# Pooling of batch 0 reordered, the sums of E folded by GpSimd, and the first linear-term operand built earlier

## The chip, the cores and the metric

The kernel runs on one core of a Trainium2 chip. The metric is the device time of one execution in microseconds. A profile of one execution gives the traces. A run's mean clock is the mean granted clock of TensorE.

Engines are named as in the profile: PE is TensorE's matmul, PEld its weight load, DVE is VectorE, ACT is ScalarE, POOL is GpSimd. Every run of the experiments is marked as in the fast state, so fast runs are compared with fast runs throughout. A line number such as L543 is a line of the kernel profiled; the same statement has another number in another kernel.

## The reference, cut to what matters

```python
def mab(q, kv):                      # attention of q on kv
    s = scale * (q @ kv.transpose(0, 2, 1))
    a = np.exp(s - s.max(-1, keepdims=True)); a /= a.sum(-1, keepdims=True) + 1e-09
    return a @ kv
h = mab(inducing, x)                 # pooling: 32 rows h for each of 4 batches
y = mab(x, h)                        # x: 4 x 12544 x 128
out = np.maximum(y @ w1, y @ w2) @ w_out      # 128 -> 1024 -> 128
```

The kernel uses max(a, b) = a + relu(b - a). The linear term, y @ w1 @ w_out, needs only a small matrix per batch (m1, and its block-diagonal form m1d); the relu term needs hwd = h @ (w2 - w1). So each batch is pooled to h, h is turned into hwd and m1, and then the large part runs: a *burst* of matmuls, relu evictions of four PSUM banks by DVE and ACT (the matmuls write into PSUM; an eviction reads a bank out and frees it: at 97.76 us of the profile before, PE has waited 0.32 us for a relu eviction of DVE), and *finals*, groups of sixteen 128x128 matmuls. Batches 1 to 3 are pooled between the bursts of the batch before. Batch 0 has nothing to hide behind.

Of the kernel before, what the change touches and what calls it, by code (L numbers as in the profile page):

```python
# [10 lines left out]
F32 = mybir.dt.float32  # L11
# [40 lines left out]
def kernel(  # L52
# [9 lines left out]
    nc = tc.nc  # L62
    B, N, C = x.shape
    M = inducing.shape[0]
# [5 lines left out]
    P1B = 16  # L70
# [4 lines left out]
    for i, (_, n) in enumerate(p1_blocks):  # L75
        step = 8 if i == NP1 - 2 else n
        units += [(i, g, min(step, n - g)) for g in range(0, n, step)]
    units = units[:-3] + units[-1:] + units[-3:-1]
    NU = len(units)
# [5 lines left out]
    smp = ctx.enter_context(tc.tile_pool(name="smp", bufs=2))  # L85
# [8 lines left out]
    model = Model()  # L94
# [14 lines left out]
    def xn_of(b, i):  # L109
        return xn_tiles[(NP1 * b + i) % NXN]  # L110
# [45 lines left out]
    with tc.manual_schedule(engines={ET.PE, ET.DVE, ET.Activation, ET.Pool, ET.SP}):  # L156
# [21 lines left out]
        st = [dict() for _ in range(B)]  # L178
# [4 lines left out]
        def u_transpose(i):  # L183
            t, g0, n = units[i]
            xn = xn_of(0, t)
            step = 4 if i == NU - 1 else 8
            for g in range(g0, g0 + n, step):
                m = min(step, g0 + n - g)
                bi, ps = bank([128, 8, 128], F16)
                end = 0.0  # L190
                for j in range(m):
                    nc.tensor.transpose(ps[:, j, :], xn[:, g + j, :], identity16)  # L192
                    end = model.pe(0.056)
                k = p1_blocks[t][0] + g
                dst = xT_tiles[0][:, k : k + m, :]
                if (g // step) % 2 == 0:
                    nc.vector.tensor_copy(out=dst, in_=ps[:, 0:m, :])  # L197
                    model.bank_free[bi] = model.ev("DVE", 64 * m, end)
                else:
                    nc.scalar.copy(out=dst, in_=ps[:, 0:m, :])  # L200
                    model.bank_free[bi] = model.ev("ACT", 128 * m, end)

        def u_scores(i):
            t, g, n = units[i]
            k = p1_blocks[t][0] + g
            bi, ps = bank([128, P1B * M])
            for j in range(n):
                nc.tensor.matmul(
                    out=ps[:, j * M : (j + 1) * M],
                    lhsT=xT_tiles[0][:, k + j, :],  # L210
                    rhs=inducingT,
                    start=True,
                    stop=True,
                )
                end = model.pe(0.025, model.bank_free[bi])
            et = etp.tile([128, P1B, M], F16, name=f"et_0_{i}", tag="et")
            nc.scalar.activation(
                out=et[:, 0:n, :], in_=ps[:, 0 : n * M], func=AF.Exp, scale=scale
            )
            model.bank_free[bi] = model.ev("ACT", n * M, end)  # L220
            pool0["et", i] = et
# [96 lines left out]


        def small_fold(b):  # L320
            es = smp.tile([128, 1, M], F32, name=f"esum_{b}", tag="esum")
            nc.vector.reduce_sum(  # L322
                out=es[:, 0, :],
                in_=st[b]["eacc"].rearrange("p k m -> p m k"),
                axis=mybir.AxisListType.X,
            )
            model.ev("DVE", P1B * M, 0.0)
            st[b]["esum"] = es[:, 0, :]

        def small_h(b):  # L330
            es = st[b]["esum"]
# [36 lines left out]
        mask = consts.tile([128, 4, 1], F16, name="mask")  # L368

        def small_m1(b):  # L370
            bi, ps = bank([128, 512])
            nc.tensor.matmul(
                out=ps[:, 0:128], lhsT=st[b]["hT4"], rhs=w1out, start=True, stop=True
            )
            end = model.pe(0.06, model.bank_free[bi])
            m1, m1d = m1_tiles[b % 2], m1d_tiles[b % 2]
            nc.scalar.copy(out=m1, in_=ps[:, 0:128])
            model.bank_free[bi] = model.ev("ACT", 128, end)
            nc.gpsimd.tensor_mul(
                m1d,  # L380
                m1[:, None, :].broadcast_to((128, 4, 128)),
                mask.broadcast_to((128, 4, 128)),
            )
            st[b]["m1"], st[b]["m1d"] = m1, m1d


# [55 lines left out]
        class Part:  # L442
# [6 lines left out]
                self.nburst = NJB // self.jpb // (2 if blk.dup else 1)  # L449
                self.name = f"{blk.name}_{t0}"  # L450

            def burst(self, u, lead=()):

                blk, w, jpb = self.blk, self.w, self.jpb
                if u == 0:
                    self.relu = relup.tile(
                        [128, NJB, blk.g, self.tn, 128], F16, name=f"relu_{self.name}", tag="relu"
                    )
                banks = []
                end = 0.0  # L460
                for q in range(4):
                    bi, ps = bank([128, 512])
                    banks.append((bi, ps, jpb * (q // 2 if blk.dup else u)))
                    free = model.bank_free[bi]
                    model.bank_free[bi] = 1e9
                    end = model.pe(0.0, max(free, blk.ready), "row")
                for jj in range(jpb):
                    for q in range(4):
                        bi, ps, j0 = banks[q]
                        jb = j0 + jj  # L470
                        r = slice(32 * q, 32 * (q + 1))
                        nc.tensor.matmul(  # L472
                            out=ps[:, jj * w : (jj + 1) * w],
                            lhsT=st[blk.b]["hwd"][r, 128 * jb : 128 * (jb + 1)],
                            rhs=blk.e2[r, 128 * self.t0 : 128 * self.t0 + w],
                            start=True,
                            stop=True,
                            tile_position=(32 * q, 0),
                        )
                end = model.pe(0.22, 0.0, "row")  # L480
                for part, q in lead:
                    part.open_final(q)
                for s in range(2):
                    for part, q in lead:
                        r = slice(32 * q, 32 * (q + 1))
                        tt = part.t0 + s
                        nc.tensor.matmul(  # L487
                            out=part.fin[q][1][:, 128 * s : 128 * (s + 1)],
                            lhsT=part.blk.e2[r, 128 * tt : 128 * (tt + 1)],
                            rhs=st[part.blk.b]["m1"][r, :],  # L490
                            start=(s == 0),
                            stop=False,
                            tile_position=(32 * q, 0),
                        )
                    if lead:
                        model.pe(0.056, 0.0, "row")
                for q in range(4):
                    bi, ps, j0 = banks[q]
                    eng = model.pick(512, end)
                    dst = self.relu[:, j0 : j0 + jpb, q % blk.g, :, :]  # L500
                    src = ps.rearrange("p (j t c) -> p j t c", j=jpb, c=128)
                    if eng == "DVE":
                        nc.vector.tensor_scalar(  # L503
                            out=dst, in0=src, scalar1=0.0, scalar2=None, op0=ALU.max
                        )
                    else:
                        nc.scalar.activation(out=dst, in_=src, func=AF.Relu)  # L507
                    self.done = model.bank_free[bi] = model.ev(eng, 512, end)
# [110 lines left out]
        def prep_w1out():  # L619
# [10 lines left out]
            nc.scalar.copy(out=w1out, in_=ps[:, 0:128])  # L630
            model.bank_free[bi] = model.ev("ACT", 128, end)

        last = NU - 3
        for i in range(last - 1):
            u_transpose(i)
            if i >= 1:
                u_scores(i - 1)
            if i >= 2:
                u_accum(i - 2)
            keep_warm(1)  # L640

        u_transpose(last - 1)
        u_scores(last - 2)
        u_transpose(last)
        u_transpose(last + 1)
        u_scores(last - 1)
        u_transpose(last + 2)
        u_accum(last - 3)
        u_scores(last)
        u_scores(last + 1)  # L650
        u_scores(last + 2)
        for i in range(last - 2, NU):
            u_accum(i)
        for i in range(NXN - NP1):
            load_x(1, i)
# [34 lines left out]
        for b in range(B - 1):  # L690
            nb, g = b + 1, first[b]
# [15 lines left out]
        for g, (p, u) in enumerate(seq):  # L707
            lead = []
            if len(queue) > 1 and queue[0][0].tn == 2 and queue[0][1] % 2 == 0:
                lead = queue[0:2]  # L710
            p.burst(u, lead)
            for blk in stages.get(g, ()):
                blk.stage()
            if g == 0:
                small_m1(0)
            if queue:
                part, *a = queue.pop(0)
                part.final(*a)
            if u == 0 and p.t0 == 0:
                p.blk.dens()  # L720
            for f, *a in jobs.pop(g, ()):
                f(*a)
            if u == p.nburst - 1:
                queue += p.finals()
# [34 lines left out]
```

## The kernel before: what the change and the argument touch

```python
        def u_transpose(i):                    # batch 0: PE transposes of unit i, evicted to xT
            ...
            step = 4 if i == NU - 1 else 8
            for g in range(g0, g0 + n, step):
                ...                            # here and below, lines of `model` are cut
                if (g // step) % 2 == 0:
                    nc.vector.tensor_copy(out=dst, in_=ps[:, 0:m, :])
                else:
                    nc.scalar.copy(out=dst, in_=ps[:, 0:m, :])
        # u_scores(i): matmuls with xT and exp on ACT; u_accum(i): sum and h accumulated on PE
        ...
        def small_fold(b):                     # E: the exponentials of the scores; sum over its 16 groups, batches 1 to 3
            es = smp.tile([128, 1, M], F32, name=f"esum_{b}", tag="esum")
            nc.vector.reduce_sum(out=es[:, 0, :],
                in_=st[b]["eacc"].rearrange("p k m -> p m k"), axis=mybir.AxisListType.X)
            model.ev("DVE", P1B * M, 0.0)
            st[b]["esum"] = es[:, 0, :]
        ...
        def small_m1(b):
            ... # PE: ps = hT4 * w1out
            nc.scalar.copy(out=m1, in_=ps[:, 0:128])
            nc.gpsimd.tensor_mul(m1d, m1[:, None, :].broadcast_to((128, 4, 128)),
                                 mask.broadcast_to((128, 4, 128)))
        ...
        last = NU - 3
        for i in range(last - 1):
            u_transpose(i)
            if i >= 1:
                u_scores(i - 1)
            if i >= 2:
                u_accum(i - 2)
            keep_warm(1)                       # one idle 128x512 matmul
        ... # the tail: see the diff
        u_h()                                  # DVE: reduce, reciprocal, h normalised
        for i in range(4):                     # w21 = w2 - w1, needed by hwd
            eng = nc.vector if i == 3 else nc.gpsimd
            sl = slice(256 * i, 256 * (i + 1))
            eng.tensor_sub(w21[:, sl], w2f[:, sl], w1f[:, sl])
        ...
            p.burst(u, lead)
            for blk in stages.get(g, ()):
                blk.stage()
            if g == 0:
                small_m1(0)
```

The program's order is fixed by hand: each engine executes in the order of the text. (In the profile before, PE is through with the m1 matmul at 27.28 us, and ACT copies it out at 28.16, behind the two relus and the exp that stand ahead of the copy in the text.) `model` is a small clock that picks the PSUM bank and the evicting engine.

The softmax here doesn't subtract the row's maximum and nothing guards it: scores larger than these inputs give would overflow.

## Time and profile before

| | before |
|---|---|
| time, three runs before the prediction | 343.66, 343.75, 344.76 us |
| span of the profiled run | 342.9 us, mean clock 0.995 |
| PE / DVE / ACT / POOL busy | 97% / 87% / 79% / 25% |
| chain that ended last | 80% PE |

PE is the bound nearly everywhere. A change that leaves PE's work alone can gain only where PE stands still or runs at half clock: eight finals take 1.06 us at 29.68, where the clock is 0.50, and 0.61 us at 32.98, where it is 1.00. There are few such places, and the prediction shows their lines: the end of batch 0's pooling (20 to 24 us), the wait for m1d with the half clock after it (28 to 33 us), and the first fold (95 to 98 us).

### The profile page before, as it was taken

Reading aid. Unit: us, or ns where it says so; the run is one execution under the profiler, and the core shown is the slowest. Engines: PE = TensorE matmul, PEld = TensorE weight load, DVE = VectorE, ACT = ScalarE, POOL = GpSimd, SP = SyncE. Lnnn points to the kernel's source line nnn. Section 1 sums busy time; section 2 is a strip of 40 time slices with the busy share of each in tenths; the row PEclk is TensorE's granted clock in tenths of the full one; section 3 lists DMA queues with packets and bytes.
Section 4 is the critical chain, followed back from the end, with each engine's and each line's share of the span. In section 5 each row is a group of like instructions: output and inputs, shape, how many; then the busy total and the mean of one; then the engine's idle time right before and its main releaser. Section 6 shows DMA issues by size and latency. Waiting matters only on the chain.

```text
span 342.9 us, 14479 instructions
## 1 busy us (share of the span) xinstructions
PE 331.4 (97%) x6346; PEld 265.3 (77%) x6346; DVE 298.5 (87%) x622; ACT 270.0 (79%) x523; POOL 87.2 (25%) x148
## 2 busy tenths in 40 slices
PE   8798999999999999999999999999999999999996
PEld 3686688888767878888777887887777887877876
DVE  1346999999889999999999999999998998989994
ACT  1656987777788877877888887777889888889882
POOL 7243121355322132643212222324212100000000
PEclk9998999999999999999999999999999999999999
DMA  7999599599917993996227992122122222222222
GB/s 132 211 270 214 132 255 219 157 195 207 221 68 155 278 224 80 189 247 176 94 94 139 266 210 96 65 94 94 69 88 95 80 94 94 96 94 94 96 96 107
DMA packets 53423, 50.42 MB, mean 147 GB/s; under 512 B 41456, under 2 KB 42128, under 8 KB 53360
## 3 DMA queue, kind: packets, MB, share of 16 engines
q0 software_dynamic: 11408, 33.43, 37.2%
q1 hardware_dynamic: 41952, 16.08, 21.1%
q8 instruction: 49, 0.80, 1.0%
q14 instruction: 14, 0.11, 0.1%
HBM read 27.28 MB, written 25.69 MB: 154 GB/s over the span
## 4 chain that ended last, share of the span: by engine, by line
PE 80%; issue 6%; POOL 4%; DMA 4%; DVE 3%; ACT 2%; POOLq 0%; ACTq 0%; DVEq 0%
PE ps L543 51%; PE ps L472 17%; DMA xn<-in_x_dram 4%; PE ps L487 4%; PE ps L407 2%; PE ps L297 2%; PE ps L275 2%; ACT relu L507 2%; POOL xn L114 1%; DVE relu L503 1%; POOL xn L119 1%; DVE o L559 1%; POOL out_dram L569 1%; PE ps L534 1%; DVE esum L322 1%
## 5 line engine op out<-in xcount | busy, mean ns | idle before, releaser
L507 ACT ACTIVATE relu<-ps 128x512 f16<-128x512 f32 x445 | 235.6, 601 | 47.5 <-PE ps L472 35.1
L503 DVE TENSOR_SCALAR relu<-ps 128x512 f16<-128x512 f32 x339 | 218.4, 680 | 5.4 <-PE ps L472 4.2
L543 PE MATMUL ps<-woutp,relu 128*128 128x128 f16 x3136 | 210.3, 220 | 0.5 <-issue 0.5
L543 PEld LDWEIGHTS <-relu 128*128 128x128 f16 x3136 | 177.3, 98 | 31.6 <-issue 21.8
L559 DVE TENSOR_TENSOR o<-ps,rp 128x256 f32<-128x256 f32 x196 | 82.0, 418 | 16.9 <-PE ps L543 12.9
L472 PE MATMUL ps<-e,hwd 32*128 32x256 f16 (+1 forms) x1632 | 83.3, 270 | 1.0 <-DVE relu L503 0.3
L569 POOL DMA_DIRECT2D out_dram<-o x75 | 41.1, 549 | 165.4 <-DVE o L559 112.1
L472 PEld LDWEIGHTS <-hwd 32*128 32x128 f16 x1632 | 27.4, 92 | 19.9 <-issue 4.1
L487 PE MATMUL ps<-m,e 32*128 32x128 f16 x372 | 29.7, 214 | 1.2 <-DVE relu L503 0.6
L487 PEld LDWEIGHTS <-e 32*128 32x128 f16 x372 | 18.4, 92 | 7.4 <-issue 4.2
L317 POOL TENSOR_TENSOR eacc<-eacc,et 128x512 f32<-128x512 f32 (+1 forms) x18 | 18.5, 1029 | 0.3
L284 ACT ACTIVATE et<-ps 128x512 f16<-128x512 f32 (+1 forms) x21 | 11.4, 545 | 4.7 <-PE ps L275 4.7
L417 ACT ACTIVATE e<-ps 128x512 f16<-128x512 f32 (+2 forms) x30 | 14.8, 546 | 0.0
L200 ACT COPY xT<-ps 128x1024 f16<-128x1024 f16 (+1 forms) x6 | 5.7, 942 | 11.1 <-PE ps L192 11.1
L114 POOL DMA_DIRECT2D xn<-in_x_dram x21 | 11.5, 550 | 5.0 <-DMA xn<-in_x_dram 4.4
L197 DVE COPY xT<-ps 128x1024 f16<-128x1024 f16 (+2 forms) x8 | 4.9, 608 | 7.7 <-PE ps L192 7.7
L297 PE MATMUL ps<-et,xn 128*128 128x32 f16 x294 | 10.7, 176 | 0.0
L275 PE MATMUL ps<-inducingT,xT 128*128 128x32 f16 x294 | 10.6, 176 | 0.0
L297 PEld LDWEIGHTS <-xn 128*128 128x128 f16 x294 | 9.6, 96 | 0.1
L275 PEld LDWEIGHTS <-xT 128*128 128x128 f16 x294 | 9.6, 96 | 0.0
L407 PE MATMUL ps<-xT,hT 128*32 128x512 f16 (+2 forms) x120 | 8.7, 349 | 0.6 <-DVE w L660 0.4
L192 PE MATMUL ps<-identity,xn 128*128 128x128 f16 x98 | 6.7, 220 | 2.5 <-DMA xn<-in_x_dram 2.2
(65 smaller groups left out, 112.8 us busy)
## 6 DMA issues: line engine op xcount, KB each, us to landing
out_dram<-o POOLq DMA_DIRECT2D x72, 256.0 KB, 3.2
xn<-in_x_dram POOLq DMA_DIRECT2D x23, 512.0 KB, 9.3
out_dram<-o SPq DMA_DIRECT2D x24, 256.0 KB, 2.0
wf<-in_moe_w_dram POOLq DMA_DIRECT2D x2, 512.0 KB, 13.8
xn<-in_x_dram POOLq DMA_DIRECT2D x2, 256.0 KB, 13.5
out_dram<-o POOLq DMA_DIRECT2D x3, 128.0 KB, 5.4
xT<-xn SPq DMA_TRANSPOSE x21, 5.9
xn<-in_x_dram POOLq DMA_DIRECT2D x4, 64.0 KB, 8.8
```

Source lines behind the costliest of these rows:

```text
L114: nc.gpsimd.dma_start(out=xn_of(b, i)[:, 0:n, :], in_=xr[b, :, k0 : k0 + n, :])
L275: nc.tensor.matmul(out=ps[:, j * M : (j + 1) * M], lhsT=xT_tiles[b % 2][:, k0 + j, :], rhs=inducingT, start=True, stop=True,)
L297: nc.tensor.matmul(out=ps[:, 0:M], lhsT=xn[:, j, :], rhs=et[:, j, :], start=(j == 0), stop=(j == n - 1),)
L317: nc.gpsimd.tensor_add(out=acc, in0=acc, in1=et[:, 0:n, :])
L407: nc.tensor.matmul(out=ps[32 * q : 32 * (q + 1), 0 : self.width], lhsT=st[self.b]["hT4"][:, 32 * q : 32 * (q + 1)], rhs=xT[:, q % self.g], ...
L472: nc.tensor.matmul(out=ps[:, jj * w : (jj + 1) * w], lhsT=st[blk.b]["hwd"][r, 128 * jb : 128 * (jb + 1)], rhs=blk.e2[r, 128 * self.t0 : 12 ...
L487: nc.tensor.matmul(out=part.fin[q][1][:, 128 * s : 128 * (s + 1)], lhsT=part.blk.e2[r, 128 * tt : 128 * (tt + 1)], rhs=st[part.blk.b]["m1" ...
L503: nc.vector.tensor_scalar(out=dst, in0=src, scalar1=0.0, scalar2=None, op0=ALU.max)
L507: nc.scalar.activation(out=dst, in_=src, func=AF.Relu)
L543: nc.tensor.matmul(out=o, lhsT=self.relu[:, jb, q, tt, :], rhs=woutp[:, jb, :], start=False, stop=(s == 1 and jb == NJB - 1),)
L559: nc.vector.tensor_mul(self.osb[:, h : h + 2, :], ps[:, 0:256].rearrange("p (s c) -> p s c", s=2), rp.broadcast_to((128, 2, 128)),)
L569: eng.dma_start(out=outr[blk.b, :, k : k + nst, :], in_=self.osb[:, 0:nst, :])
```

## The change

Its intent: leave less work behind the last load of batch 0; take a reduction off the busy VectorE; let PE start the first finals sooner. Cut to its core:

```diff
@@ u_transpose
-            step = 4 if i == NU - 1 else 8
+            step = 8
-                if (g // step) % 2 == 0:
+                if i >= NU - 3 or (g // step) % 2 == 0:
@@ small_fold
-            nc.vector.reduce_sum(out=es[:, 0, :], in_=st[b]["eacc"]...)
-            model.ev("DVE", P1B * M, 0.0)
+            acc = st[b]["eacc"]
+            n = P1B // 2
+            while n:
+                nc.gpsimd.tensor_add(out=acc[:, 0:n, :], in0=acc[:, 0:n, :], in1=acc[:, n : 2 * n, :])
+                n //= 2
@@ small_m1: the product in two halves
-            nc.gpsimd.tensor_mul(m1d, ...)
+            for q in (0, 2):
+                nc.gpsimd.tensor_mul(m1d[:, q : q + 2, :], ...)
@@ burst: `between()` is called after the matmuls and ahead of the relu evictions
@@ pooling of batch 0
             u_transpose(i)
             if i >= 1:
-                u_scores(i - 1)
-            if i >= 2:
-                u_accum(i - 2)
+                u_accum(i - 1)
+            u_scores(i)
             keep_warm(1)
         u_transpose(last - 1)
-        u_scores(last - 2)
+        u_accum(last - 2)
         ...
         u_transpose(last + 2)
-        u_accum(last - 3)
+        u_accum(last - 1)
         ...
-        for i in range(last - 2, NU):
+        for i in range(last, NU):
             u_accum(i)
@@ first burst
-            p.burst(u, lead)
+            p.burst(u, lead, (lambda: small_m1(0)) if g == 0 else None)
...
-            if g == 0:
-                small_m1(0)
```

I call the parts A (pooling of batch 0), B (fold) and C (operand), as the prediction does.

More of the change, by code (lines that the diff above doesn't have):

```diff
@@ L320, in small_fold @@
         def small_fold(b):
-            es = smp.tile([128, 1, M], F32, name=f"esum_{b}", tag="esum")
-            nc.vector.reduce_sum(
-                out=es[:, 0, :],
-                in_=st[b]["eacc"].rearrange("p k m -> p m k"),
-                axis=mybir.AxisListType.X,
-            )
-            model.ev("DVE", P1B * M, 0.0)
-            st[b]["esum"] = es[:, 0, :]
+            acc = st[b]["eacc"]
[3 more added lines that the diff above has]
+                n //= 2
+            st[b]["esum"] = acc[:, 0, :]
         def small_h(b):
@@ L378, in small_m1 @@
             model.bank_free[bi] = model.ev("ACT", 128, end)
-            nc.gpsimd.tensor_mul(
-                m1d,
-                m1[:, None, :].broadcast_to((128, 4, 128)),
-                mask.broadcast_to((128, 4, 128)),
-            )
+            for q in (0, 2):
+                nc.gpsimd.tensor_mul(
+                    m1d[:, q : q + 2, :],
+                    m1[:, None, :].broadcast_to((128, 2, 128)),
+                    mask[:, q : q + 2, :].broadcast_to((128, 2, 128)),
+                )
             st[b]["m1"], st[b]["m1d"] = m1, m1d
@@ L450, in __init__, with burst @@
                 self.name = f"{blk.name}_{t0}"
-            def burst(self, u, lead=()):
+            def burst(self, u, lead=(), between=None):
                 blk, w, jpb = self.blk, self.w, self.jpb
@@ L496, in burst @@
                         model.pe(0.056, 0.0, "row")
+                if between:
+                    between()
                 for q in range(4):
```

## The prediction

Where the text is marked as cut, it told of the hardware what no run of this case shows; one cut takes out half of the second rival's cause. Its sum: 0.1 (A) + 1.1 (B) + 0.95 (C) = 2.15 us, from 343.75 to 341.6 us. That its 18 final matmuls of 1.9 us would take half at full clock is in the trace: from 29.62 to 31.49 us at 0.50, the next 18 from 32.92 to 33.92 at 1.00.

> **What bounds the kernel now.** I read the page first: which engine is full, and where it is not.
>
> ```profile
> PE 331.4 (97%) x6346; PEld 265.3 (77%) x6346; DVE 298.5 (87%) x622; ACT 270.0 (79%) x523; POOL 87.2 (25%) x148
> ...
> PEclk9998999999999999999999999999999999999999
> ```
>
> TensorE (PE) is busy 97% of the 342.9 us span, and the chain that ended last is 80% PE. From about 39 us on it runs groups of sixteen 1.00 us matmuls almost without a hole, so a microsecond saved before that, or a hole closed later, should come off the end one for one. The change adds and removes almost no PE work; it can only pay by closing holes. The fourth slice of the clock row is below full, so I looked there next, with the timeline: how the pooling of batch 0 ends, then how the first block starts. Columns are start, length, engine, line, output<-inputs, and in brackets the idle time ahead with its releaser.
>
> ```profile
> 17.35 1.07 PE L192 MATMUL ps<-identity,xn 128*128 128x128 f16 x16 [1.09 <-DMA xn<-in_x_dram]
> ...
> 20.09 0.62 PE L192 MATMUL ps<-identity,xn 128*128 128x128 f16 x8 [0.20 <-DMA xn<-in_x_dram]
> ...
> 21.17 0.60 PE L208 MATMUL ps<-inducingT,xT 128*128 128x32 f16 x18
> ...
> 23.57 0.29 DVE L253 TENSOR_REDUCE hrec<-ps 128x32 f32<-128x128 f32 x1 [2.62 <-PE ps L233]
> ```
>
> The last load lands at 20.09 and h is only normalised at 23.57: 3.48 us of transposes, scores and accumulation stand behind the last byte.
>
> ```profile
> 28.16 0.28 ACT L377 CAST m<-ps 128x128 f16<-128x128 f32 x1
> ...
> 28.53 1.03 POOL L379 TENSOR_TENSOR m1d<-m,mask 128x512 f16<-128x512 f16 x1 [1.67 <-ACT m L377]
> 29.62 0.27 PE L534 MATMUL ps<-m1d,e 128*128 128x128 f16 x1 [1.18 <-POOL m1d L379]
> ```
>
> PE stands 1.18 us for m1d, the linear-term operand. Its matmul had started at 27.05, but ScalarE copied it out only after two relus and an exp, and GpSimd then took 1.03 us.
>
> ```profile
> 25.90:29.31 3.41, 2.27 (x50) 1.47 (x47) 2.62 (x7) 3.24 (x10) 1.74 (x3) 1.00 1.08 217
> 29.31:32.72 3.41, 3.10 (x43) 2.56 (x42) 1.38 (x4) 0.66 (x2) 0.52 (x2) 0.50 1.05 210
> ```
>
> These are two stretches (us, then busy time of PE, weight load, DVE, ACT, POOL, then the granted clock). After the stretch with the hole, the clock is 0.50 for 3.41 us, while DVE and ACT starve. Last, the fold of E in batches 1 and 2:
>
> ```profile
> 94.80 0.32 POOL L317 TENSOR_TENSOR eacc<-eacc,et 128x64 f32<-128x64 f32 x1
> ...
> 95.15 1.03 DVE L322 TENSOR_REDUCE esum<-eacc 128x32 f32<-128x512 f32 x1 [1.11 <-POOL eacc L317]
> ...
> 96.32 0.38 PE L333 MATMUL ps<-esum,ones 128*128 128x32 f32 x2
> ...
> 97.76 0.37 PE L472 MATMUL ps<-e,hwd 32*128 32x256 f16 x5 [0.32 <-DVE relu L503]
> ```
>
> VectorE waits 1.11 us in order for GpSimd and then reduces for 1.03 us; relu evictions queue behind it and PE runs out of banks.
>
> [...] here a 128x256 subtraction takes 725 ns on POOL and 461 on DVE, 1.57 times. So the fold moves to the slower engine on purpose: POOL is at 25%.
>
> **Part A, pooling of batch 0.** The PE order becomes transpose i, accumulate i-1, score i. What is left behind the last load is one accumulation, three scores and three accumulations instead of one, three and five: 2 x 0.62 us (4 sum matmuls of 0.056 and 16 of 0.0245) leave the tail. That would be 1.24 us. But scoring unit i now waits for its own evictions. From a unit's first transpose, ACT's eviction starts 1.09 us later and takes 1.01, so the second half of the scores starts at +2.12, ends at +2.32, and the warming matmul (0.215) makes the cycle 2.55 us. Loads land every 2.45 us. From the first transpose at 7.78 the next units would start at 10.33 (data ready at 9.07), 12.88, 15.43 and 17.98, against 17.35 now: the 3.4 us gap in the loads absorbs only part of the lag. Then: accumulate unit 3 to 19.50, ten transposes to 20.06, scores of unit 4 to 20.46, last transposes to 20.91. The exp of unit 4 ends near 21.28 and its accumulation near 21.95; the last scores end at 22.40. Three exps follow in line on ACT (0.86 us in the trace) from 22.22 to 23.08; the last accumulation then has its sums at 23.24, plus 0.22 of latency: h starts at 23.46 instead of 23.57. So A is worth about **0.1 us**, and I allow -0.5 to +0.4. All evictions of the last three units on DVE (one of 0.69 instead of 0.42 beside 0.59) fall inside the waits.
>
> **Part B, the fold.** Three DVE reductions go (1.03, 0.95, 0.95 us; the group's mean is 972 ns). POOL gets four adds of 256, 128, 64 and 32 columns. From 1171 ns for 512 columns and 318 for 64, one add is about 196 + 1.904n ns: 684, 440, 318, 257, in sum 1.70 us. Batch 1: eacc ends at 95.12, the fold at about 96.95, and PE comes to its sum matmul at 96.3: a new wait of 0.7 us. Now this round of PE, from 95.27 to the next group of final matmuls at 98.29, takes 3.02 us where its work (1.0 + 0.38 + 0.33 + 0.1) is 1.8; so 1.2 is lost now and 0.7 after, gain 0.5. In batches 2 and 3 the instruction order puts an output DMA ahead of the fold, which waits for VectorE until 172.01; the fold ends at 174.4 and PE asks at 175.70: no wait. There the DVE reduction costs PE 0.28 us of measured wait. Gain 0.3 each. B: **1.1 us**, allowed 0.4 to 1.3.
>
> **Part C, the operand of the first block.** Its matmul now follows burst 0 directly and its copy precedes the relus on ACT. It needs w1out, ready at 26.87 in the present trace; so matmul from 26.92, copy 27.19 to 27.46, ACT's relus to 28.00 and 28.55 (0.45 later than now). POOL finishes issuing loads at 26.86, so the half product starts at 27.5 and takes about 0.6 (1.04 us for both halves now, plus one more fixed cost). It is there at 28.1. The final matmul then waits for DVE's second relu at 28.25 instead: 28.35 against 29.62, 1.27 us sooner. Not all of it arrives: with the copy and exp ahead of burst 1's relus, ACT is busy to 30.05. Today the next burst's relus reach ACT at 32.27; at full clock PE would have done its 18 final matmuls in half of their 1.9 us, so about 31.0. Gain **0.95 us** against a run of the old kernel at full clock, 2.2 against one that dropped it.
>
> **Which of the two is the time before?** Three runs gave 343.66, 343.75 and 344.76; the profiled one, which dropped the clock, 344.69. An estimate from the trace is that the drop costs about 1.1 us, and 1.0 separates those pairs. I take it that the median has no drop. Sum: 0.1 + 1.1 + 0.95 = 2.15 us, 343.75 - 2.15 = **341.6 us**.
>
> **The rivals.** First, A works as meant: the PE keeps pace with the loads and the tail is about 0.7 us shorter; then 341.0. For it: exps of the last units are small. Against it: the 2.55 us cycle against 2.45. Second, the new PE wait for GpSimd's chain takes all that B frees in batch 1, [...]; then 342.5. For it: 96.95 against 96.3, and the adds are serial. Third, the lag in A grows through the 20 us before the last load, or delays the small kernels' start, and PE idles enough for more clock drops: 343. Fourth, the old kernel's fast runs all hold the clock drop and the new one's do not: 340.4. Nothing makes an engine other than PE the bound: DVE gives up 2.9 us of work and POOL rises by some 5 us to 27%.
>
> **Range and chances.** The errors of A (0.5), B (0.4) and C (0.6 with the clock) give about 1.3 us either way: **340.2 to 343.0**. Faster by over 2% would need 336.9, more than three times the sum: 0.02. Within 2%: 0.97. Slower by over 2% would need 350.6: 0.01.
>
> **What the changed profile would show.** A: the fifth unit's 16 transposes start near 18.0 rather than 17.35, and the normalising reduction near 23.5. If the transposes start at 17.4, the lag is wrong. B: no DVE reduction on eacc; four POOL adds in 1.7 us; the first sum matmul waits some 0.7 us, the later two do not. C: the first m1d matmul about 1.2 us sooner after burst 0 and waiting for a relu instead of POOL; no stretch at 0.50 near 30 us. What would make the prediction wrong is above all the clock: a drop in the new kernel that the old fast runs lack adds about 1 us; and a reordered ACT queue that opens a hole elsewhere.

## The result, and the profile after

| | before | after |
|---|---|---|
| median of 6 runs | 343.71 us | 340.56 us |
| all runs | 343.40 to 344.85 | 340.09 to 341.17 |
| profiled span, mean clock | 342.9, 0.995 | 338.5, 1.000 |

The ratio is 0.9901, with a 95% interval of 0.9881 to 0.9921. Ratios here are the mean time of one kernel's fast runs over that of the other's of the same rounds, so not quite the ratio of the medians quoted. The gain is clear, and below 2%.

The page of the kernel after, its busy line and its clock row:

```profile
PE 329.7 (97%) x6346; PEld 263.8 (78%) x6346; DVE 295.9 (87%) x620; ACT 269.7 (80%) x521; POOL 92.9 (27%) x164
...
PEclk9999999999999999999999999999999999999999
```

DVE lost 2.6 us of work and POOL gained 5.7, but PE's share is what it was. The clock row has no dent now. The timeline after, for part A (start, length, engine, line, what, and in brackets the idle time ahead with its releaser):

```profile
18.19 1.05 PE L192 MATMUL ps<-identity,xn 128*128 128x128 f16 x16
...
20.66 0.61 PE L192 MATMUL ps<-identity,xn 128*128 128x128 f16 x8
...
22.12 0.60 PE L208 MATMUL ps<-inducingT,xT 128*128 128x32 f16 x18
...
23.62 0.29 DVE L253 TENSOR_REDUCE hrec<-ps 128x32 f32<-128x128 f32 x1 [1.62 <-PE ps L233]
```

The fifth unit starts at 18.19 instead of 17.35, and the normalising reduction at 23.62 instead of 23.57: it is no earlier. For part C:

```profile
26.86 0.27 ACT L375 CAST m<-ps 128x128 f16<-128x128 f32 x1 [0.30 <-PE ps L370]
...
27.21 1.18 POOL L378 TENSOR_TENSOR m1d<-m,mask 128x256 f16<-128x256 f16 x2 [0.37 <-ACT m L375]
...
27.99 0.23 PE L535 MATMUL ps<-m1d,e 128*128 128x128 f16 x1
```

The first m1d matmul is at 27.99 instead of 29.62, and no longer waits for POOL. For part B, the folds of batches 1 and 2:

```profile
91.62 1.99 POOL L324 TENSOR_TENSOR eacc<-eacc 128x256 f32<-128x256 f32 x4
...
93.66 0.41 PE L331 MATMUL ps<-eacc,ones 128*128 128x32 f32 x2 [0.97 <-POOL eacc L324]
...
168.87 2.00 POOL L324 TENSOR_TENSOR eacc<-eacc 128x256 f32<-128x256 f32 x4
...
171.50 0.36 PE L331 MATMUL ps<-eacc,ones 128*128 128x32 f32 x2
```

In batch 1, PE waits 0.97 us for POOL's chain of adds; in batch 2 POOL is done 0.6 us ahead.

**Where the 4.4 us between the two profiles come from.** Both kernels scale their outputs with 196 equal DVE instructions, so the start of the nth one is a common ruler. I read the starts from the two timelines and subtracted:

| scaled output no. | before | after | difference | gained since the row above |
|---|---|---|---|---|
| 5 | 41.70 | 38.96 | 2.74 | 2.74 (start-up, A, C and clock) |
| 29 | 79.79 | 77.06 | 2.73 | 0.0 |
| 36 | 91.89 | 88.32 | 3.57 | 0.84 |
| 49 | 113.67 | 109.96 | 3.71 | 0.14 (first fold) |
| 113 | 216.47 | 212.46 | 4.01 | 0.30 (second fold) |
| 161 | 291.16 | 286.71 | 4.45 | 0.44 (third fold) |
| 196 | 339.78 | 335.35 | 4.43 | 0.0 |

The 0.84 us between outputs 29 and 36 belong to nothing in the change. The timeline of the kernel before has a hole there:

```profile
85.31 0.62 PE L543 MATMUL ps<-woutp,relu 128*128 128x128 f16 x8
86.46 0.61 PE L543 MATMUL ps<-woutp,relu 128*128 128x128 f16 x8 [0.53 <-issue]
```

A group of sixteen final matmuls is torn in two, with no wait for any engine or DMA ("issue" is time for which the profile shows no cause). No other profile has it there: output 36 comes 11.25 to 11.31 us after output 29 in all of them, 12.10 in this one. So a single profile of before overstates the gain, and the pair alone cannot tell how much of the first 2.74 us is A, C or the clock. The experiments do that.

### The profile page after: what moved, and what is told of

Read it like the earlier page. It is cut to its first block, busy times and chain, and to the rows that moved or that the text cites. A ratio compares the mean times of both kernels' runs of the same rounds, so it can differ in the third digit from the quotient of the medians.

```text
span 338.5 us, 14493 instructions
## 1 busy us (share of the span) xinstructions
PE 329.7 (97%) x6346; PEld 263.8 (78%) x6346; DVE 295.9 (87%) x620; ACT 269.7 (80%) x521; POOL 92.9 (27%) x164
## 4 chain that ended last, share of the span: by engine, by line
PE 93%; ACT 3%; DVE 1%; POOL 1%; issue 1%; DVEq 0%; POOLq 0%
PE ps L544 56%; PE ps L471 19%; PE ps L486 4%; PE ps L297 2%; PE ps L275 2%; PE ps L406 2%; PE ps L173 2%; PE ps L192 2%; ACT relu L508 1%; ACT xT L200 1%; PE ps L208 1%; PE ps L427 1%; PE ps L350 1%; DVE relu L504 1%; POOL eacc L324 1%
## 5 line engine op out<-in xcount | busy, mean ns | idle before, releaser
L197 DVE COPY xT<-ps 128x1024 f16<-128x1024 f16 (+1 forms) x8 | 5.1, 642 | 8.4 <-PE ps L192 8.4
L200 ACT COPY xT<-ps 128x1024 f16<-128x1024 f16 x5 | 5.1, 1012 | 9.0 <-PE ps L192 9.0
L173 PE MATMUL ps<-warm 128*128 128x512 f16 x22 | 7.7, 495 | 1.2 <-DVE warm L158 1.2
```

## The experiments

Twelve kernels ran, each on one chip and with runs of before. All gave correct results. I quote medians, the ratio to before with its interval, and the clocks.

### Set one: one part at a time, and the clock alone

**Only A**: the two hunks of `u_transpose` and those of "pooling of batch 0", nothing else.

> The kernel before with the pooling order of batch 0 alone (accumulate unit i-1, then score unit i; last three units evicted by VectorE). Theory 1, the lag of the prediction: the unit of five starts its transposes near 18.1 us instead of 17.35, the normalising reduction stays within 0.2 us of 23.57, time 343.4 to 343.8 and the half-clock stretch (mean clock 0.995) stays. Theory 2, the order works as meant: the reduction starts near 22.9 and the time is 343.0 or less.

Measured: 343.53 us, before 344.17, ratio 0.9992 (0.9963 to 1.0022). The clocks of its six runs are 0.989 to 1.000. Its waits of PE show the price of the order:

```profile
PE ps L208 <- ACT xT L200: 1.3, 4, 0.4
...
PE ps L534 <- POOL m1d L379: 1.2, 1, 1.2
```

Four times the scores of a unit stand up to 0.4 us for the eviction of their own transposes (columns: total us, times, longest). The wait for m1d is as before. Its fifth unit starts its transposes at 17.99 and the normalising reduction is at 23.42, as theory 1 has them. Nothing is gained that these runs resolve: theory 1.

**Only B**: the hunk of `small_fold`.

> The kernel before with the fold on GpSimd alone. Theory 1 (ledger of the two profiles, 0.15 + 0.30 + 0.44): 0.9 us less, about 342.8, with a PE wait of about 1 us for GpSimd in the first fold and none in the two others. Theory 2: the new wait takes it all, 343.5 or more.

Measured: 343.10 us, ratio 0.9969 (0.9937 to 1.0001). The medians are noisy (before ran from 342.55 to 345.25 here), but the ruler is not: from output 36 to 49 it takes 21.64 us against 21.78 in before, from 85 to 113 44.85 against 45.18, from 113 to 161 74.23 against 74.69. That is 0.14 + 0.33 + 0.46 = 0.93 us, and the PE wait for POOL is there once:

```profile
PE ps L331 <- POOL eacc L324: 1.0, 1, 1.0
```

So theory 1 holds: the wait takes back most of the first fold's gain and none of the others'.

**Only C**: `between`, and the two halves.

> The kernel before with the early operand copy and its product in two halves alone. Theory 1, the old kernel's fast runs all hold the half-clock stretch and this one's do not: 2 us or more less, 341.7 or lower, mean clock 1.000 against 0.995. Theory 2, the old fast runs hold no such stretch: about 1 us less, 342.7, and the clocks of the fast runs are equal.

Measured: 341.74 us, ratio 0.9947 (0.9917 to 0.9977). Five of six runs have a clock of 0.999 or 1.000, one 0.995. Before's eleven runs beside it:

| mean clock | runs of before, us |
|---|---|
| 0.999 to 1.000 | 342.55, 342.92, 343.20, 343.47, 344.47 |
| 0.993 to 0.995 | 343.65, 344.17, 344.57 |
| 0.989 to 0.990 | 344.85, 345.15, 345.25 |

Neither theory is right as it was written. The old fast runs do not *all* drop the clock; they draw lots. One stretch of 3.41 us at half clock takes 0.005 off the mean over the span (3.41 x 0.5 / 342.9), so I read the three rows as none, one and two such stretches; that is an estimate, as no run of the third row was profiled. (The run of 344.47 shows that other things cost a microsecond too, as the hole above does. A mean of 0.998 is not a drop: the profile of both edits, further down, has it, and there the clock is full to 336.12 us and halved only from there to the end at 337.24, when the last scaled output, started at 334.15, is done.)

**The clock alone.** The kernel before, with idle matmuls in PE's wait for m1d:

```diff
+            if g == 1:
+                i = sorted(range(8), key=lambda j: model.bank_free[j])[1]
+                fill = psum.tile([128, 512], F32, name=..., tag=f"bank{i}", bufs=1)
+                for _ in range(4):
+                    nc.tensor.matmul(out=fill, lhsT=warm[:, 0:128], rhs=warm, start=True, stop=True)
             if queue:
                 part, *a = queue.pop(0)
                 part.final(*a)
```

> The kernel before with four idle 128x512 matmuls put on PE between burst 1 and the first output matmuls, inside its 1.18 us wait for m1d; nothing else moves. Theory 1, the clock drop is caused by that idle stretch and costs about 1.1 us in every fast run: about 342.6, mean clock 1.000, m1d wait still ending near 29.6. Theory 2, the drop does not cost the end anything, since VectorE and ScalarE are the limit there: 343.7 with the clock at 1.000. Theory 3, one microsecond of work is too little to keep the clock: 343.7 and 0.995.

Measured: 342.85 us, ratio 0.9969 (0.9942 to 0.9997), and all six clocks are 0.999 or 1.000. Its timeline and its two windows, to be set against the two windows that the prediction shows of before (us, then busy time of PE, weight load, DVE, ACT and POOL, clock, DMA share, GB/s):

```profile
28.09 1.04 PE L721 MATMUL ps<-warm 128*128 128x512 f16 x4
29.33 0.22 PE L534 MATMUL ps<-m1d,e 128*128 128x128 f16 x1 [0.20 <-POOL m1d L379]
```

```profile
25.60:29.00 3.40, 3.12 (x54) 1.78 (x51) 2.61 (x7) 3.32 (x10) 1.97 (x4) 1.00 1.05 212
29.00:32.40 3.40, 3.09 (x61) 2.50 (x59) 2.34 (x6) 1.78 (x5) 0.88 (x2) 1.00 1.05 212
```

The m1d matmul waits just as long: from the first matmul of burst 0 to it 29.33 - 26.21 = 3.12 us, as in before (29.62 - 26.50). Only the clock differs: it stays at 1.00 afterwards. None of the six filled runs has a drop, while six of the eleven unfilled ones beside them have one or two. So in these runs filling the wait removes the drop, and four matmuls that compute nothing save what the half clock costs: theory 1, except for its "every fast run".

What decides whether an unfilled run drops is shown only in part. The packed traces record when the clock changes. In all four profiles with a drop (before, only A, only B, and "batch 1 one burst later" below) the half clock begins 23.89 us after the start of the first stretch at full clock, and lasts 3.41 (3.413 in before, and 23.89 is seven times that). In before the full clock then holds for 310.61 us, 91 times 3.413; in the changed kernel's first profile it holds for 334.51 us, 98 times, and changes only after PE's last matmul. So the changes recorded in these profiles lie on a grid of 3.41 us counted from the start of the full clock. Where burst 0 falls on it differs from execution to execution. In the three profiles with a drop that have the long m1d wait, it begins 0.1 to 0.6 us after a line of that grid; in the two profiles of the old order of the copy that have no drop (filled, and the halves alone below) it begins 2.28 and 1.78 us after one. So the filled profile alone could have escaped by its place; the evidence is the six clocks, and that four profiles with part C lie 0.16 to 0.55 us after a line and have no drop. PE's busy time in the 3.41 us ahead does not decide by itself. The stretches ahead of those three drops have 2.27, 2.04 and 1.96 us of it, but these two stretches, of before and of only C, were not followed by half clock either:

```profile
15.66:19.07 3.41, 2.32 (x57) 2.02 (x53) 0.80 (x2) 1.53 (x3) 1.06 (x2) 1.00 1.12 232
16.22:19.64 3.42, 1.81 (x42) 1.78 (x42) 0.85 (x2) 1.02 (x2) 1.06 (x2) 1.00 1.10 273
```

### Set two: the changed kernel again, and two edits of it

**The changed kernel once more**, now with before's clocks listed.

> The changed kernel once more, now beside runs of the kernel before whose clocks are listed. Theory 1, the parts add up and the rest is the clock: runs of before at clock 1.000 are 2 to 2.5 us above this one, those at 0.995 about 3.2, those at 0.990 about 4.3; this kernel is at 1.000 in nearly all runs, about 340.5. Theory 2, the parts help each other: even against runs of before at 1.000 the gain is 3 us or more.

Measured: 340.65 us, ratio 0.9921 (0.9897 to 0.9945), six runs from 339.93 to 341.79 with a mean of 340.63, clocks 0.998 to 1.000. Of before's eleven, the six at 1.000 have a mean of 342.66, two at 0.993 and 0.994 are 343.12 and 343.22, three at 0.989 and 0.990 are 344.22 to 344.65. Against clean runs the change is worth 342.66 - 340.63 = 2.0 us. Theory 1, at its lower edge; the runs at half clock came out 0.5 to 0.7 us faster than it said.

**Without the idle matmul per unit**: `keep_warm(1)` taken out of the pooling loop.

> The changed kernel without the one idle 128x512 matmul per unit in the pooling of batch 0. Theory 1, the unit's cycle of 2.55 us against loads every 2.45 is what eats the gain of the new order: the cycle falls to 2.37, the unit of five starts its transposes at 17.4 instead of 18.2, the normalising reduction comes at 22.9 to 23.1 instead of 23.6, and the time falls by 0.3 to 0.6 us. Theory 2, the small products behind it wait for other things (the subtraction on GpSimd to 24.75, the output weights), so the reduction is earlier but the end is not: within 0.2 us. Theory 3, PE is too idle without them and a clock drop comes in: slower, clock 0.995 or less.

Measured: 340.69 us, ratio 0.9920 (0.9899 to 0.9942): no change against the kernel above. The cycle of a unit fell from 2.59 to 2.37 us, but in the profiled execution the first transposes happened to begin 0.8 us later (8.44 us, against 7.63 in the changed kernel's second profile), so this trace alone decides nothing. It does not refute theory 2 either; the last edit of this set shows more.

**Batch 1 one burst later**:

```diff
-            for s, f in ((40, small_fold), (42, small_h), (43, small_hwd), (44, small_m1)):
+            late = 1 if b == 0 else 0
+            for s, f in ((40, small_fold), (42 + late, small_h), (43 + late, small_hwd), (44 + late, small_m1)):
```

> The changed kernel with the sum matmul, the products and the operand of batch 1 one burst later, so that GpSimd's fold is done. Theory 1, the PE wait of 0.97 us in the first fold is lost time: it goes, and the time falls by 0.6 to 0.9 us. Theory 2, PE only catches up there with evictions that it would wait for anyway: within 0.2 us.

Measured: 339.69 us, ratio 0.9894 (0.9868 to 0.9920), in the same rounds that gave the changed kernel 0.9921. The intervals overlap; the traces decide. In this kernel's timeline the fold and the sum matmul are

```profile
93.30 1.99 POOL L324 TENSOR_TENSOR eacc<-eacc 128x256 f32<-128x256 f32 x4
...
95.64 0.36 PE L331 MATMUL ps<-eacc,ones 128*128 128x32 f32 x2
```

with no wait, and from output 36 to 85 it takes 78.12 us against 79.26 in the changed kernel's second profile: 1.1 us less. Theory 1, with more than the 0.6 to 0.9 that it said. Two of its six runs, the profiled one among them, show the clock at 0.994. This drop lies elsewhere: the half clock begins at 27.77 us, and in the window before it PE waits twice for the subtracted weights, not for m1d:

```profile
PE ps L350 <- POOL w L660: 0.9, 2, 0.5
```

In this execution the load of the weights let POOL begin the subtractions at 23.18 us (22.64 in the changed kernel). In all listed runs, 4 of 50 with C's early copy have a drop, 27 of 51 without it, and none of the 6 filled ones: the change makes the drop rarer, not impossible.

**Both edits.**

> Both of the two edits before on the changed kernel. If both help by themselves, they lie in different stages and add: 0.9 to 1.5 us below the changed kernel, 339.0 to 339.8. If neither does, 340.5.

Measured: 339.28 us, ratio 0.9888 (0.9863 to 0.9914), one of six clocks at 0.994. That is in the range set for both helping, but it does not show it: taking out the idle matmul alone gave nothing, and the step from batch 1 later (339.69) is not resolved. More telling than the time is the head of its trace, where the lag of A is gone:

```profile
22.97 1.07 PE L611 MATMUL ps<-identity,wf 128*128 128x128 f32 x8
24.11 0.24 PE L406 MATMUL ps<-xT,hT 128*32 128x128 f16 x4
24.28 0.39 PE L350 MATMUL ps<-w,hT 128*128 128x256 f16 x2
25.02 0.38 PE L350 MATMUL ps<-w,hT 128*128 128x256 f16 x2 [0.35 <-POOL w L659]
25.33 0.24 PE L406 MATMUL ps<-xT,hT 128*32 128x128 f16 x4
```

The pooling's last matmuls end 0.65 us sooner than in the changed kernel (the transposes of the weights start at 22.97 instead of 23.62), and the first matmuls on h follow at 24.11 instead of 24.75. Counted from the first transposes (7.58 here, 7.84 there) the order is worth 0.39 us of it; the rest is the start of the execution. Then the third product with w21 waits for POOL, which subtracts the weights after they land. (POOL starts those subtractions at 22.65 here and at 22.64 in the changed kernel, there after 4.14 us of waiting for the DMA of the weights: the load sets it.) The next step starts at 25.33, where it started at 25.46 in the changed kernel: of 0.65 us, 0.13 is left, less than the shift of the start.

### Set three: A taken out, C split, and the wait behind A moved

**The changed kernel without A** (B and C alone).

> The changed kernel with the old pooling order: fold and operand changes alone. Theory 1, the new pooling order is worth nothing because of its lag and of the subtraction behind it: within 0.3 us of the changed kernel, about 340.6 where before is 342.7 at clock 1.000. Theory 2, it is worth the 0.5 us that the ledger of its own run shows early on: about 341.1.

Measured: 340.28 us, ratio 0.9913 (0.9892 to 0.9934), four runs, all at clock 1.000. The changed kernel itself had 0.9901 and 0.9921. A is worth nothing that can be seen: theory 1.

**C, the order alone** (one product of 1.03 us) and **C, the halves alone** (the copy still behind the relus).

> The kernel before with the operand matmul and its copy put ahead of the relu evictions, the product still one GpSimd instruction of 1.04 us. Theory 1, the order is the larger part: m1d comes near 28.3 instead of 29.6, 0.3 us after the relus are ready, so 0.3 to 0.4 us less gain than both halves of the part together, about 342.0 where before is 342.7 to 343.0 at clock 1.000; fewer clock drops. Theory 2, without the halves the PE still waits long enough to drop the clock as often as before.

> The kernel before with the product in two halves alone, the copy still behind two relus and an exp. The first half is there 0.45 us sooner (near 29.15): 0.3 to 0.5 us less time than before at the same clock, and the half-clock stretch still in most runs.

Measured: order 341.59 us, ratio 0.9953 (0.9933 to 0.9973), all six clocks 1.000; halves 342.29 us, ratio 0.9976 (0.9953 to 0.9999), clocks 0.994 and 0.995 in two of six. The first m1d matmul in the timeline of each:

```profile
28.05 0.22 PE L536 MATMUL ps<-m1d,e 128*128 128x128 f16 x1 [0.24 <-POOL m1d L379]
```

```profile
28.64 0.22 PE L535 MATMUL ps<-m1d,e 128*128 128x128 f16 x1 [0.75 <-DVE relu L504]
```

The execution's start shifts by up to 0.7 us from profile to profile, so I measure from the start of burst 0's matmuls:

| profile | burst 0 | burst 0 to first m1d matmul | burst 0 to output 5 | clock from 29 to 32 us |
|---|---|---|---|---|
| before | 26.50 | 3.12 | 15.20 | half |
| before, filled | 26.21 | 3.12 | 14.07 | full |
| halves alone | 25.95 | 2.69 | 13.64 | full |
| order alone | 25.94 | 2.11 | 13.06 | full |
| only C | 26.63 | 1.80 | 12.77 | full |
| changed | 26.19 | 1.80 | 12.77 | full |
| changed without A | 26.34 | 1.80 | 12.77 | full |

This table is the core of the matter. At full clock every tenth that the first m1d matmul comes sooner arrives at output 5: 0.43 for the halves, 1.01 for the order, 1.30 (14.07 - 12.77) for both, and the half clock costs 15.20 - 14.07 = 1.13 us on top. The order is the larger part, as expected; that its runs never dropped the clock speaks against theory 2. The halves alone brought the first half 0.43 us sooner (0.45 expected), but "in most runs" missed for the half clock: two of six. The start of burst 0 itself lies between 25.94 and 26.63 with the old pooling and at 25.98, 25.99 and 26.19 with the new one: A moved nothing there that these profiles resolve. With this the first row of the ruler can be split: 2.74 us = 1.30 (C) + 1.13 (clock) + 0.31 (burst 0 at 26.19 instead of 26.50, within that scatter).

**The subtractions shared two and two**, on the kernel with both edits:

```diff
+        sub(nc.vector, 0)
         u_h()
-        for i in range(4):
-            eng = nc.vector if i == 3 else nc.gpsimd
+        sub(nc.gpsimd, 1)
+        sub(nc.gpsimd, 2)
+        sub(nc.vector, 3)
```

> The last kernel of the set before (no idle matmul per unit, batch 1 one burst later) with the four subtractions of the weights shared two and two: VectorE takes the first one before it normalises h. Theory 1, GpSimd's three subtractions after the landing of the second weight (to 24.75 us) are what the first small products wait for once h is early: the products no longer wait, 0.4 to 0.7 us less than that kernel (339.3), about 338.8. Theory 2, something later (operand, load issues on GpSimd to 26.8) takes its place: 339.3.

Measured: 338.99 us (338.30 to 339.28, four runs, clocks 1.000), ratio 0.9873 (0.9851 to 0.9896). It has the lowest ratio of all, but the kernel with both edits had 0.9888 on another chip with overlapping intervals, so a step of 0.3 us is not resolved. Between 22 and 27 us its PE waits once, and for another thing:

```profile
PE ps L406 <- DVE hT L260: 0.6, 1, 0.6
```

The products no longer wait for POOL, but h comes later, since VectorE now subtracts first. Theory 2 is nearer in kind: the wait moved. That kernel beats the old one clearly, 1.27% below before against 0.8 to 1.0%, and also the changed one without A on the same chip: 338.30 to 339.28 us against 340.02 to 340.39.

## Why the prediction was right or wrong

The time was in the range, 1.0 us below the middle, where the range had room because it allowed for the clock. By its own steps:

- **A, right in outcome, half right in cause.** It said 0.1 us. The cycle of a unit is 2.59 us (2.55 predicted), the fifth unit starts at 18.19 (near 18.0 predicted), the reduction at 23.62 (23.46 predicted). So the lag was read correctly from the instruction order. What it missed is that A had a second lid: with the lag gone, the products wait for the subtracted weights, whose load had been seen in the trace ("POOL w L660" started only at 22.65) and not followed. That lid did not bind in the changed kernel itself, so the 0.1 did not depend on it.
- **B, right in kind, a little too large.** It said 0.5 + 0.3 + 0.3 = 1.1 us. The ruler says 0.14 + 0.30 + 0.44 = 0.88. The chain of adds takes 1.99 us, not 1.70: the four adds have 0.73, 0.45, 0.32 and 0.25, sum 1.75, and about 0.08 passes between each and the next, which depends on it. PE's wait became 0.97 instead of 0.7, and the first gain shrank to 0.14. So the chain takes twice the 0.97 us of the DVE reduction that it replaces, and the move still gains; the likely reason, the author's estimate from the profile before, is that POOL was busy 25% of the span and DVE 87%, and that PE there waited 0.32 us for a relu that stood behind the reduction.
- **C, the mechanism right, the size too small at full clock.** The m1d matmul came 1.32 us sooner after burst 0; 1.27 was predicted. The term that was off is the deduction after it: "Not all of it arrives", with 0.95 left because ACT was said to be busy with burst 1's relus. All of it arrived, 1.30. In the trace after, ACT is done with burst 1's relus at 29.37, 3.18 us after burst 0 starts (the working had 30.05 - 26.50 = 3.55), and takes the next burst's first relu at 29.54, 3.35 us after; in the filled kernel before that was 4.65 (30.86 - 26.21). For the case with a clock drop it said 2.2; measured is 15.20 - 12.77 = 2.43.
- **The sum for clean runs** was 2.15 us. Against before's clean runs the changed kernel gains 2.0 in the second set.
- **The step that failed is "Which of the two is the time before?"** It took the median of before as free of the drop, with the second level, 1 us up, as the drop. Its 1.1 us for one drop was right (1.13 in the traces). But the clocks listed later show three levels, and of 33 runs of before only 16 are clean by their mean clock, 11 have one drop and 6, as read above, two. (The levels overlap: in the third set two clean runs took 343.93 and 344.00, more than any of its runs with one drop.) The changed kernel had none in its twelve (0.998 at the lowest). So the mean gain is the 2.0 to 2.2 of the parts plus what the lots cost before: 23 drops in 33 runs, at 0.4 to 0.9 us each by the means and 1.13 by the traces, an estimate of 0.3 to 0.8 us per run. Together 2.3 to 3.0; the three comparisons of this kernel, or of it without A, gave mean gains of 2.6, 2.9 and 3.4 us. The median run of before held one drop twice (344.17, 343.13) and was clean once (342.99). For the six runs of before in the first comparison no clocks are listed. Its 3.4 would fit if its lower group, near 343.6, already held a drop. The profiled run of before, 344.69 us, speaks for it: it held one drop and the torn group, and 344.69 - 1.13 - 0.84 leaves an estimate of 342.7 for a clean run, 0.9 below that group. But for the group itself it stays open.
- **The rivals.** The first (A works as meant) fell with A alone and with A taken out. The second (POOL's chain takes B's gain) is nearly right for batch 1 alone, where 0.14 us is left. The third (the lag makes PE idle enough for more drops) did not come: four of six runs of only A have one, six of the eleven of before beside them, none of the changed kernel's. The fourth (old fast runs all drop, new ones do not) was wrong about "all" and right about the direction; its 340.4 came nearest to the 340.56 measured.

What stays open: whether the unfilled runs at 0.989 and 0.990 do hold a second stretch at half clock, and what makes it (none was profiled), what in the 3.41 us ahead of a drop decides on it, and what the torn group at 86 us is. One other profile, that of the subtractions shared two and two, has such a hole, of 0.49 us at 154 us; so its place varies.

## What to carry to other kernels

When PE is busy 97% of the time, look for what is left in two places: a short stall at which PE waits for a small operand that sits behind larger work in another engine's queue, and the half clock that such a stall can set off (six of eleven runs of before had it, none of the six with the stall filled); moving the small copy ahead of the evictions was the larger part of this change, 1.01 of the 1.30 us at output 5. Follow a chain of waits to its second lid before crediting a shorter first one: the early h met weights that were not yet subtracted. And when runs of one kernel scatter by whole steps, list the clock of every run before comparing medians: here one drop cost 1.13 us, over half of the 2.0 that the change gains between clean runs.
